# Two ranks in a kernel's opening plan: batch 0's theta earlier on TensorE, the splits of theta's weights later

## The chip, the cores and the metric

The kernel runs on one core of one Trainium2 chip. The metric is the device time in microseconds of one execution. The kernel before the change was run three times: 577.52, 577.86 and 578.83, median 577.86 us. TensorE is called PE here (PEld its weight loads), VectorE DVE, ScalarE ACT, GpSimd POOL, SyncE SP.

## What is computed

Banded attention with 8 heads of 64 dimensions feeds a block that mixes tokens with a learned rotation, for 8 batches of 576 positions:

```
scores = q k^T / 8, masked (heads 0-3: the last 32 positions; heads 4-7: every 4th of the last 128)
x      = softmax(scores) v, heads side by side: (8, 576, 512)
theta  = x w_theta                       # 512 x 512
zr, zi = x cos(theta), x sin(theta)
u      = x + w_tok_r zr + w_tok_i zi     # 576 x 576 each, over tokens
out    = u + relu(u w_ch)                # 512 x 512
```

The result is float32.

## The kernel before

Heads are worked in four pairs `pr`. For each batch and pair, `scores` multiplies q and k in bands, masks, and takes the exponentials (ACT) and the normalization (POOL). `flip` (on PE, batch 0) or `turn` (on DVE, batch 1 on) transposes the probabilities, `pv` multiplies them with v, and `x_evac` copies the result to x, which lies with 128 of the 512 dimensions on the partitions.

Theta is computed for five tiles of tokens, in the order `STS = (4, 0, 1, 2, 3)`; tile 4 has 64 tokens, the others 128. `theta0` does it for batch 0: one float32 product for each of the four pieces `c` of the 512 dimensions, into a PSUM bank named by `TP0`. When the four are done it starts `trig` for the tile. `trig` rounds theta to whole turns on ACT (K, line 787), subtracts them on DVE (line 789), and takes the sine on ACT (line 796). It also starts `natural`, four transposes on PE that bring x to tokens on partitions (xn, line 759). `by_x` multiplies sine and xn on DVE (line 750), `cosine` takes the absolute value (line 698) and the cosine (line 705) on ACT and multiplies again. `zsplit` splits each product into a rounded high part zh (DVE, line 641, or ACT, line 644) and a rest zl (POOL, line 646). There are nine such pieces `kt` for the token product: kt 0 to 3 are from cosines of tiles 0 to 3, kt 4 to 7 from their sines, kt 8 holds both of tile 4.

`token` sums over the nine pieces in the order `KORD = (0, 4, 1, 5, 2, 6, 3, 7, 8)`, three products each (zh and zl with the weights' high part, zh with their low part), for four pieces `d` of the dimensions and two halves `g` of the tokens: eight units. `residual` adds x and splits u. `chan` does the last product in eight more units and `finish` adds the result.

Weights come in as raw pairs of words and are made floats by `unpack` (a clamp on DVE, line 332; ACT, lines 334 and 340, or DVE, line 337; DVE, line 342). Then `split` makes the high part on ACT (line 350) and the rest on POOL (line 352). Theta's weights are used whole for batch 0 (`wth32`), and split (`theta_split`) for the other batches. `theta_split` for piece c may start when all five tiles have used that piece. The channel weights' split lands in the tile where the raw theta weights lay, so `chan_weights` waits for the event `("wc", c)` of `theta_split` (line 386). The token weights' second half (`token_late`) and the channel weights are loaded into tiles that earlier steps give back.

The sine and the exponential need different tables on ACT. The exponentials of batch 1 wait until the last sine or cosine of batch 0 has been issued (event `sin0`, lines 444 and 500), and `table` keeps their order.

The order of the opening (batch 0, and scores, turns, pv and theta of batch 1) is made by the planner `Order` while the program is built. Each step of work is a generator which yields an engine with an estimated cost, or an event to wait for. `run` takes the engine that can start first, and on it, among the steps that are ready by then, the one of lowest rank, and of equal ranks the one started first (line 120). It never leaves an engine idle while a step is ready. A step becomes ready again an engine-dependent latency after its end (0.1 us for PE). A step that is started by another, as `natural` by `trig`, inherits the rank unless it is given one (line 89). What was planned is pinned: each engine executes it in that order. The ranks are in `RANK`. `theta0` adds 0.01 for each tile in STS order (line 966), `trig0` too (line 670), `theta_split` and the token weights 0.01 for each piece, and scores 0.21 for each pair. PE instructions are pinned in every phase; from batch 1's token products on, the other engines' order is left to the compiler's scheduler.

Of the kernel before, what the change touches and what calls it, by code (L numbers as in the profile page):

```python
# [29 lines left out]
EARLY = ("u0", "u1", "u2", "u3", "xh0")  # L30
LATE = ("u3", "xh1", "xh2", "xh3", "xh0")
LATE2 = ("xh2", "xh3", "xh2", "xh3")
RANK = dict(load=6.64, scores0=1.09, flip=0.01, pv0=1.13, pair=.21, theta_unpack=1.54, theta0=5.3, trig0=2.41,
            token_early=2.55, theta_split=6.42, token_late=6.75, chan=2.1, units=2.95, evacuate=4.49,
            scores1=4.02, scores2=7.3, pv1=8.0, theta1=5.96, trig1=7.42)
STS = (4, 0, 1, 2, 3)

# [24 lines left out]
class Order:  # L62
# [17 lines left out]
    def signal(self, event):  # L80
        self.events[event] = self.now

    def go(self, gen, rank=None):
        if not self.live:
            for _ in gen:
                pass
            return
        self.serial += 1
        t = [self.rank if rank is None else rank, self.serial, self.now, gen, None, 0.0]
        self.tasks.append(t)  # L90
        self.advance(t)
# [60 lines left out]
def build(ctx, tc, qT, kT, vw, wth, wtk, wch, maskb, ident, identb, outT):  # L152
# [46 lines left out]
    def give(tag, n):  # L199
        if od.live:  # L200
            signal(("free", tag, n))
# [11 lines left out]
    def load_qk(n):  # L213
        if n >= B * NP:
            return
        b, pr = divmod(n, NP)
        r = yield from take("qk", 2)
        q = ap.tile([128, 2 * NJ, 2 * QB], F32, tag="q", name=f"q{b}_{pr}")
        k = ap.tile([128, S + 32], F32, tag="k", name=f"k{b}_{pr}")
        yield "DMA", dma(2 * S)  # L220
        pin(nc.sync.dma_start(q, qT[b, pr]))
        yield "DMA", dma(S + 32)
        pin(nc.sync.dma_start(k, kT[b, pr]))
        qks[b, pr] = (q, k, r)
        signal(("qk", b, pr))

    def load_va(n):
        if n >= B * NP:
            return
        b, pr = divmod(n, NP)  # L230
        r = yield from take("va", 2)
        va = ap.tile([128, VA, 128], F32, tag="va", name=f"va{b}_{pr}")
        yield "DMA", dma(VA * 128)
        pin(nc.sync.dma_start(va, vw[b, pr, :, :VA]))
        vs["a", b, pr] = (va, r)
        signal(("va", b, pr))

    def load_vb(n):
        if n >= B * NP:
            return  # L240
        b, pr = divmod(n, NP)
        if n == NP - 1:
            r = None
            vb = hp.tile([128, DM], F32R, tag="zl8", name="first_vb").bitcast(F32)
            vb = vb.rearrange("p (a b) -> p a b", b=128)
        else:
            r = yield from take("vb", 1)
            vb = ap.tile([128, NJ - VA, 128], F32, tag="vb", name=f"vb{b}_{pr}", bufs=1)
        yield "DMA", dma((NJ - VA) * 128)
        pin(nc.sync.dma_start(vb, vw[b, pr, :, VA:]))  # L250
        vs["b", b, pr] = (vb, r)
        signal(("vb", b, pr))
# [162 lines left out]
    def on_pe(b, pr):  # L415
        return b == 0 or (b, pr) in ((1, 2), (1, 3), (2, 0), (2, 1))
# [24 lines left out]
    def scores(b, pr):  # L441
# [35 lines left out]
        else:  # L477
            give("qk", rqk)
            go(load_qk(b * NP + pr + 2), RANK["load"])
        if b and on_pe(b, pr):  # L480
# [122 lines left out]
    def pv(b, pr):  # L603
# [18 lines left out]
        if ra is not None:  # L622
            give("va", ra)
            go(load_va(n + 2), RANK["load"])
        if rb is not None:
            give("vb", rb)
            go(load_vb(NP if n == NP - 2 else n + 1), RANK["load"])
        if b:
# [25 lines left out]
    def theta0(st):  # L654
        cs = slice(128 * st, min(128 * st + 128, S))
        n = cs.stop - cs.start
        for c in range(NC):
# [11 lines left out]
            signal(("th0", st, c))  # L669
        go(trig(0, st), RANK["trig0"] + .01 * STS.index(st))  # L670

# [145 lines left out]
    def residual(b, d, g, ps, rel):  # L817
        ts = slice(HS * g, HS * g + HS)
        x = xf[b, d]
        if g == 0:  # L820
            yield from take(f"u{d}", 1, UH.get(d) if b == 0 else None)
            u = hp.tile([128, 2, S], F32R, tag=f"u{d}", name=f"u{b}_{d}")
            uh[b, d], ul[b, d] = u[:, 0], u[:, 1]
        yield "DVE", dve(HS)
        pin(nc.vector.tensor_tensor(x[:, ts], ps, x[:, ts], op=ALU.add))  # L825
        give(*rel)
        yield "ACT", act(HS)
        pin(nc.scalar.copy(uh[b, d][:, ts], x[:, ts]))  # L828
        yield "POOL", pool(HS)
        pin(nc.gpsimd.tensor_tensor(ul[b, d][:, ts], x[:, ts], uh[b, d][:, ts].bitcast(F32), op=ALU.subtract))  # L830
        signal(("u", b, d, g))
# [4 lines left out]
    def token(b, d, g):  # L836
# [15 lines left out]
        signal(("tk", b, d, g))  # L852
        go(residual(b, d, g, ps, rel), RANK["evacuate"])

    def finish(b, e, g, ps, rel):
        ts = slice(HS * g, HS * g + HS)
        x = xf[b, e]
        yield "DVE", dve(HS)
        pin(nc.vector.scalar_tensor_tensor(out=x[:, ts], in0=ps, scalar=0.0, in1=x[:, ts],  # L859
                                           op0=ALU.max, op1=ALU.add))  # L860
        give(*rel)
        signal(("out", b, e, g))
        if b == B - 1:
            pin(nc.sync.dma_start(outT[b, e][:, ts], x[:, ts]))
        elif g == 1:
            yield "DMA", dma(S)
            pin(nc.sync.dma_start(outT[b, e], x))

    def chan(b, e, g):
# [7 lines left out]
        for c in range(NC):  # L877
# [3 lines left out]
            for l, r in ((wchs[c][0], uh[b, c]), (wchs[c][0], ul[b, c]), (wchs[c][1], uh[b, c])):  # L881
                pe(nc.tensor.matmul(ps, l[:, cs], r[:, ts], start=(n == 0), stop=(n == 3 * NC - 1)))  # L882
                n += 1
        go(finish(b, e, g, ps, rel), RANK["evacuate"])

# [173 lines left out]
```

## Time and profile before

| what | value |
|---|---|
| median of three runs | 577.86 us |
| the profiled execution's own time | 577.82 us |
| its span, first to last instruction | 576.0 us |
| mean granted TensorE clock | 0.988 |
| busy: PE, DVE, ACT, POOL | 550.5, 378.0, 345.2, 222.2 us |

Busy time is given as a share of a stretch of time. In the timeline views each row is a start, a length, an engine, a line of the kernel, an operation, what it writes and reads, and how many such instructions were merged; brackets hold the idle time of the engine ahead of it and what ended that. The granted clock is the share of full TensorE speed.

### The profile page before, as it was taken

What the parts mean: (1) busy time and instruction counts of PE and PEld (TensorE: products, weight loads), DVE (VectorE), ACT (ScalarE), POOL (GpSimd) and SP (SyncE); (2) the same over time, 40 slices, a digit from 0 to 9 for tenths busy, and PEclk for the clock granted to TensorE, in tenths of its full rate; (3) what the DMA queues carried; (4) which work ended last, traced back from release to release, by engine and by line L of the source; (5) the groups of instructions that cost most, each with busy time, mean ns of one, the idle gap of its engine ahead of it and who ended that gap; (6) DMA issues with size and microseconds to landing.
All of it is one profiled execution on the core that took longest, in us unless ns stands there. A gap on an engine that the chain in (4) does not pass through costs nothing.

```text
span 576.0 us, 13996 instructions
## 1 busy us (share of the span) xinstructions
PE 550.5 (96%) x5464; PEld 501.6 (87%) x5464; DVE 378.0 (66%) x1156; ACT 345.2 (60%) x939; POOL 222.2 (39%) x206
## 2 busy tenths in 40 slices
PE   5997799999999999999999999999999999999997
PEld 4744688879999899988999899988999899989997
DVE  3879798865666668756776768756775767445112
ACT  1498967768555784369555785359556695266110
POOL 2228855525224352226324253226323353325220
PEclk9999699899999999999999999999999999999999
DMA  8991437601747046540746146550747123321002
GB/s 303 400 368 28 165 105 245 216 0 63 231 150 193 32 162 210 169 127 20 268 143 172 64 148 202 181 136 11 252 146 190 69 83 102 77 89 65 18 1 83
DMA packets 45586, 81.91 MB, mean 142 GB/s; under 512 B 3920, under 2 KB 19024, under 8 KB 45520
## 3 DMA queue, kind: packets, MB, share of 16 engines
q1 hardware_dynamic: 45520, 81.02, 43.7%
q8 instruction: 43, 0.70, 0.5%
q14 instruction: 23, 0.19, 0.1%
HBM read 64.49 MB, written 16.52 MB: 141 GB/s over the span
## 4 chain that ended last, share of the span: by engine, by line
DVE 34%; ACT 30%; PE 25%; issue 5%; POOL 2%; DMA 2%; SPq 0%; ACTq 0%; POOLq 0%; DVEq 0%
DVE pt L525 16%; PE y L850 11%; ACT P L504 11%; PE c L882 6%; PE th L685 3%; DVE P L409 3%; ACT K L698 3%; ACT K L787 3%; DVE xh L599 3%; ACT th L796 2%; ACT zh L644 2%; DVE xq L729 2%; DVE K L789 2%; ACT cos L705 2%; ACT x L581 2%
## 5 line engine op out<-in xcount | busy, mean ns | idle before, releaser
L830 POOL TENSOR_TENSOR u<-x,u 128x288 fp32r<-128x288 f32 x64 | 54.7, 858 | 184.6 <-ACT u L828 184.6
L525 DVE STREAM_TRANSPOSE pt<-P 32x288 f32<-32x288 f32 x224 | 105.1, 469 | 12.0 <-POOL P L510 8.9
L882 PE MATMUL c<-u,late_wc 128*128 128x288 f32 x768 | 110.2, 296 | 2.8 <-DVE x L859 2.8
L882 PEld LDWEIGHTS c<-u,late_wc 128*128 128x128 f32 x768 | 106.0, 188 | 6.8 <-DVE x L859 4.0
L850 PE MATMUL y<-wtkh,zh 128*128 128x288 f32 x288 | 90.3, 314 | 1.1 <-ACT zh L644 1.1
L850 PE MATMUL y<-wtkh,zl 128*128 128x288 f32 x288 | 86.2, 299 | 4.0 <-POOL zl L646 4.0
L646 POOL TENSOR_TENSOR zl<-g,zh 128x512 fp32r<-128x512 f32 x40 | 52.3, 1316 | 97.5 <-ACT zh L644 84.5
L504 ACT ACTIVATE P<-P,mx 128x64 f32<-128x64 f32 x216 | 72.0, 335 | 25.8 <-DVE mx L498 25.8
L850 PE MATMUL y<-wtkl,zh 128*128 128x288 f32 x288 | 85.9, 298 | 0.0
L828 ACT CAST u<-x 128x288 fp32r<-128x288 f32 x64 | 26.9, 429 | 86.2 <-DVE x L825 85.5
L685 PE MATMUL th<-wthh,xh 128*128 128x512 f32 x224 | 74.8, 395 | 0.3 <-DVE g L784 0.3
L850 PE MATMUL y<-late_wt_b,zh 128*128 128x288 f32 x320 | 68.1, 297 | 0.0
L825 DVE TENSOR_TENSOR x<-y,x 128x288 f32<-128x288 f32 x64 | 28.1, 448 | 53.6 <-PE y L850 53.5
L850 PEld LDWEIGHTS y<-wtkh,zl 128*128 128x128 f32 x288 | 55.1, 191 | 4.7 <-POOL zl L646 4.7
L850 PEld LDWEIGHTS y<-wtkh,zh 128*128 128x128 f32 x288 | 54.9, 191 | 4.7 <-ACT zh L644 2.3
L850 PE MATMUL y<-late_wt_a,zh 128*128 128x288 f32 x256 | 56.3, 301 | 0.0
L850 PEld LDWEIGHTS y<-wtkl,zh 128*128 128x128 f32 x288 | 55.1, 191 | 0.3 <-issue 0.3
L510 POOL TENSOR_TENSOR P<-P,sm 128x576 f32<-128x576 f32 x32 | 37.5, 1172 | 41.1 <-DVE sm L508 18.1
L850 PEld LDWEIGHTS y<-late_wt_b,zh 128*128 128x128 f32 x320 | 51.4, 189 | 0.3
L685 PEld LDWEIGHTS th<-wthh,xh 128*128 128x128 f32 x224 | 42.0, 188 | 9.2 <-DVE g L784 0.6
L850 PE MATMUL y<-late_wt_b,zl 128*128 128x288 f32 x160 | 47.4, 296 | 0.0
L581 ACT COPY x<-o 128x576 f32<-128x576 f32 x32 | 29.4, 919 | 28.4 <-PE o L617 19.1
(108 smaller groups left out, 1106.3 us busy)
## 6 DMA issues: line engine op xcount, KB each, us to landing
q<-in_qT_dram SPq DMA_DIRECT2D x32, 576.0 KB, 5.2
va<-in_vw_dram SPq DMA_DIRECT2D x30, 320.0 KB, 3.2
k<-in_kT_dram SPq DMA_DIRECT2D x28, 304.0 KB, 5.5
out_dram<-x SPq DMA_DIRECT2D x28, 288.0 KB, 2.4
vb<-in_vw_dram SPq DMA_DIRECT2D x29, 256.0 KB, 3.8
xd<-xq SPq DMA_DIRECT2D x24, 288.0 KB, 5.1
xn<-xd SPq DMA_DIRECT2D x24, 256.0 KB, 3.4
st_wtk<-in_wtk_dram SPq DMA_DIRECT2D x8, 576.0 KB, 8.8
```

The lines of the kernel that those rows point to most:

```text
L409: pin(nc.vector.tensor_tensor_reduce(out=P[:, n], in0=ps[:, n - g0], in1=mskb[:, mask_of(pr, n)], op0=ALU.add, op1=ALU.max, scale=1.0, sca ...
L504: table(nc.scalar.activation(P[:, n], P[:, n], AF.Exp, bias=mx[:, n:n + 1], scale=SCALE, accum_out=sm[:, n:n + 1]))
L510: pin(nc.gpsimd.tensor_tensor(P, P, sm.unsqueeze(2).to_broadcast([128, NJ, BW]), op=ALU.mult))
L525: pin(nc.vector.transpose(pmats[b, pr][k0:k0 + QB, :, hh, QB * e:QB * e + QB], P[p0:p0 + QB, :, QB * o:QB * o + QB]))
L581: pin(nc.scalar.copy(dst, src))
L646: pin(nc.gpsimd.tensor_tensor(lo, z, hi.bitcast(F32), op=ALU.subtract))
L685: pe(nc.tensor.matmul(pt, l, r, start=(n == 0), stop=(n == 3 * NC - 1)))
L825: pin(nc.vector.tensor_tensor(x[:, ts], ps, x[:, ts], op=ALU.add))
L828: pin(nc.scalar.copy(uh[b, d][:, ts], x[:, ts]))
L830: pin(nc.gpsimd.tensor_tensor(ul[b, d][:, ts], x[:, ts], uh[b, d][:, ts].bitcast(F32), op=ALU.subtract))
L850: pe(nc.tensor.matmul(ps, l[:, cs], r, start=(n == 0), stop=(n == 3 * NK - 1)))
L882: pe(nc.tensor.matmul(ps, l[:, cs], r[:, ts], start=(n == 0), stop=(n == 3 * NC - 1)))
```

## The change

Two entries of `RANK` get other values. `theta0` goes from 5.3 to 2.39: above 2.39 are now `trig0` (2.41, with the transposes of `natural`), `token_early` (2.55), `units` (2.95, the token and channel products) and `scores1` (4.02 and up), which were below 5.3. `theta_split` goes from 6.42 to 8.74: `load` (6.64), `token_late` (6.75), `scores2` (7.3), `trig1` (7.42) and `pv1` (8.0 to 8.63) are now below it. Nothing else differs; the same instructions are issued in another order.

```diff
-RANK = dict(load=6.64, scores0=1.09, flip=0.01, pv0=1.13, pair=.21, theta_unpack=1.54, theta0=5.3, trig0=2.41,
-            token_early=2.55, theta_split=6.42, token_late=6.75, chan=2.1, units=2.95, evacuate=4.49,
+RANK = dict(load=6.64, scores0=1.09, flip=0.01, pv0=1.13, pair=.21, theta_unpack=1.54, theta0=2.39, trig0=2.41,
+            token_early=2.55, theta_split=8.74, token_late=6.75, chan=2.1, units=2.95, evacuate=4.49,
             scores1=4.02, scores2=7.3, pv1=8.0, theta1=5.96, trig1=7.42)
```

## The prediction

> **What bounds the kernel now.** I read the page's busy table first, then the busy time by stage, then the order of time on TensorE, ScalarE and VectorE in the stage that the change touches.
>
> ```profile
> PE 550.5 (96%) x5464; PEld 501.6 (87%) x5464; DVE 378.0 (66%) x1156; ACT 345.2 (60%) x939; POOL 222.2 (39%) x206
> ```
>
> Over the whole span TensorE (PE) is the bound. By stage (columns: stretch, its length, busy us of PE, PEld, DVE, ACT, POOL, granted clock, DMA share, GB/s) it is not the same everywhere:
>
> ```profile
> 50.00:69.90 19.90, 13.78 (x98) 10.58 (x97) 16.39 (x50) 18.44 (x54) 17.52 (x15) 0.78 0.41 136
> 69.90:120.00 50.10, 47.05 (x539) 42.52 (x537) 44.94 (x101) 34.86 (x119) 28.41 (x25) 0.95 0.48 163
> 143.00:560.00 417.00, 414.22 (x4083) 390.61 (x4083) 265.44 (x898) 244.60 (x692) 151.30 (x145) 1.00 0.42 129
> ...
> 37.82:61.28 23.46, 19.55 (x116) 10.90 (x116) 21.66 (x48) 21.28 (x39) 18.06 (x13) 0.92 0.40 139
> ```
>
> From 143 us on PE is idle 2.8 us in 417 (417.00 - 414.22): whatever PE arrives early at that point is kept to the end, one for one. Before it, from 50 to 69.9, PE is idle 6.1 us of 19.9 at a granted clock of 0.78, while ScalarE (ACT) is busy 18.4 of 19.9. That is the stage of batch 0's sines and cosines, and the change works there. From 69.9 to 120 VectorE (DVE, 44.9 of 50.1) and PE (47.1) are both nearly full; this stage can be started earlier but hardly shortened.
>
> TensorE's order of time in the first stage (start us, us, line, names, entries; a theta product L667 shows as two entries):
>
> ```profile
> 36.30 2.21 PE L667 MATMUL th<-st_wth,x 128*64 128x512 f32 x4 [0.56 <-ACT x L581]
> 38.34 0.60 PE L759 MATMUL xn<-idt,x 128*64 128x128 f32 x4
> 38.78 1.97 PE L667 MATMUL th<-st_wth,x 128*128 128x512 f32 x4
> 40.59 0.60 PE L759 MATMUL xn<-idt,x 128*128 128x128 f32 x4
> 41.02 1.97 PE L667 MATMUL th<-st_wth,x 128*128 128x512 f32 x4
> 42.91 0.80 PE L468 MATMUL s<-k,q 128*64 128x64 f32 x20
> 43.65 2.07 PE L667 MATMUL th<-st_wth,x 128*128 128x512 f32 x4
> 45.56 0.60 PE L759 MATMUL xn<-idt,x 128*128 128x128 f32 x4
> 45.99 3.77 PE L667 MATMUL th<-st_wth,x 128*128 128x512 f32 x8
> 49.60 0.60 PE L759 MATMUL xn<-idt,x 128*128 128x128 f32 x4
> ...
> 52.09 1.06 PE L667 MATMUL th<-st_wth,x 128*128 128x512 f32 x2
> ...
> 53.38 1.06 PE L667 MATMUL th<-st_wth,x 128*128 128x512 f32 x2
> ...
> 56.52 0.41 PE L850 MATMUL y<-wtkh,zl 128*128 128x288 f32 x1 [1.52 <-POOL zl L646]
> ...
> 66.79 0.40 PE L850 MATMUL y<-wtkh,zl 128*128 128x288 f32 x1 [1.11 <-POOL zl L646]
> ```
>
> The reader should see two things. Theta's last product ends at 54.4 because transposes, scores and token products stand between its pieces. And from 50 us on PE waits for z (zl from GpSimd, POOL), which comes out of the sine chain.
>
> **The change part by part.** *Theta forward on TensorE.* From 36.30 on there are 28 theta entries, so 14 products, of 3.77/4 = 0.94 us: 13.2 us. The new ranks step by 0.01: theta of the tiles in STS order stands at 2.39 to 2.43, each tile's transposes at 2.41 to 2.45 (they inherit trig's rank, line 89), and line 120 gives a tie to the task that was there first. So the transposes of tile 4 come behind theta of tiles 4, 0 and 1, but ahead of tiles 2 and 3; those of tile 0 only ahead of tile 3. One tile's next product becomes ready 0.1 us after its last, in the planner's terms, so products of two tiles alternate. This gives: five products, transposes of tile 4 at 41.0; two products, transposes of tile 0 at 43.4 (one transpose group takes 45.99 - 45.56 = 0.43); six products, transposes of tile 1 at 49.5; one product, theta ends at 36.3 + 13.2 + 3 x 0.43 = 50.8. Against 54.4 that is 3.6 us earlier. The first half of scores (0.74 us at 42.91), tokens and the transposes of tile 2 come after it.
>
> Are the transposes missed? They move from 38.34, 40.59 and 45.56 to 41.0, 43.4 and 49.5. Their readers are the products x times sine on DVE:
>
> ```profile
> 41.65 0.69 DVE L750 TENSOR_TENSOR g<-xn,g 64x512 f32<-64x512 f32 x1
> ...
> 43.77 0.69 DVE L750 TENSOR_TENSOR g<-xn,g 128x512 f32<-128x512 f32 x1
> ...
> 50.59 0.68 DVE L750 TENSOR_TENSOR g<-xn,g 128x512 f32<-128x512 f32 x1
> ```
>
> Ended at 41.5, 43.9 and 49.9 the transposes meet these starts to within 0.1 us. They cost nothing as long as the sines themselves don't come sooner; when that cover is gone each microsecond counts on DVE.
>
> *What the earlier theta is worth.* Not 3.6 us, because PE does not set this stage:
>
> ```profile
> 50.70 0.45 ACT L350 CAST wtkh<-st_wtk 128x288 fp32r<-128x288 f32 x1 [1.48 <-DVE st_wtk L342]
> ...
> 51.59 0.65 ACT L350 CAST wthh<-st_wth 128x512 fp32r<-128x512 f32 x1
> ...
> 55.95 0.58 ACT L787 ACTIVATE K<-th 128x512 int32<-128x512 f32 x1
> ...
> 58.39 0.63 ACT L796 ACTIVATE g<-K 128x512 f32<-128x512 f32 x1 [0.68 <-DVE K L789]
> ...
> 60.66 0.71 ACT L705 ACTIVATE K<-K,halfpi 128x512 f32<-128x512 f32 x1
> ...
> 62.03 1.28 ACT L504 ACT_TABLE_LOAD   x1
> ```
>
> The rounding K of the last tile starts at 55.95, 1.5 us after its theta is done, and ACT is not idle in front of it: it stands in ACT's queue. The last cosine starts at 60.66; behind it comes the table load at 62.03 and all exponentials of batch 1, which wait for the last sine or cosine (line 500). From 37.82 (first K) to 61.28 ACT is busy 21.28 of 23.46 us. What can leave this stretch: the idle 2.18 us, and the four casts of theta's weights, which the second edit ranks last.
>
> *Theta's split behind all else.* It moves four casts on ACT and four subtractions on POOL:
>
> ```profile
> L350 ACT CAST wthh<-st_wth 128x512 fp32r<-128x512 f32 x4 | 2.6, 654 | 0.0
> L352 POOL TENSOR_TENSOR wthl<-st_wth,wthh 128x512 fp32r<-128x512 f32 x4 | 5.3, 1323 | 0.0
> ```
>
> The planner never leaves an engine idle while something is ready, so a cast can still fill a short gap early; it yields only where the unpacking of the second half of the token weights (6.75 to 6.79) is ready, now ranked ahead. I take two of the four casts as leaving the stretch: 1.3 us. Bounds: none (0, or the token unpacking takes the same place) and all four (2.6). Of the idle time the 0.68 us wait for L789 of the last tile goes, since that tile's theta and K come sooner and L789 has a place further ahead in DVE's queue. The 1.48 us wait hangs on a slow DVE operation of the token weights, not on theta; I take half, 0.7, between none and all. The sum is 0.7 + 0.7 + 1.3 = 2.7 us, between 0.7 and the full 2.18 + 2.6 = 4.8.
>
> Is DVE able to follow? In the same stretch it is busy 21.66 of 23.46. It is relieved, since masking of batch 1's first scores moves behind with the scores, but it holds the gain below 4 us. On POOL the split's products stand among the zl ones; two 1.3 us pieces in front of the last zl vanish, which agrees with zl following ACT's casts.
>
> One cost in this stage is contention of DVE with POOL:
>
> ```profile
> L332 DVE TENSOR_SCALAR st_wtk<-st_wtk 128x576 f32<-128x576 f32 x6 | 4.2, 703 | 0.0
> L332 DVE TENSOR_SCALAR st_wtk<-st_wtk 128x288 f32<-128x288 f32 x2 | 2.9, 1456 | 0.0
> ```
>
> Half as many words take twice as long, in a stage where POOL is full. Against 0.70 for the larger form a meeting costs at least 0.8 us. If packing the zl products closer makes two more such meetings, 1.6 of the 2.7 us are lost. I keep that as the low end of the gain (1.1) and take no more meetings than before as the likelier, since the number of operations on both engines is unchanged. [...]
>
> *Who waits for theta's split.* The channel weights overwrite its raw tile (line 386), and batch 1's theta needs the split.
>
> ```profile
> 69.80 1.30 POOL L352 TENSOR_TENSOR wthl<-st_wth,wthh 128x512 fp32r<-128x512 f32 x1
> ...
> 95.99 0.66 ACT L350 CAST late_wc<-st_wch 128x512 fp32r<-128x512 f32 x1
> ...
> 71.00:96.00 25.00, 23.95 (x319) 21.45 (x320) 22.40 (x50) 18.33 (x62) 14.30 (x14) 1.00 0.47 163
> ```
>
> The last piece ends at 71.1 and the first reader is at 95.99. In these 25 us ACT has 6.7 and POOL 10.7 us free, which hide 2.6 and 5.3. I cost this at nothing; without the cover up to 5.3. No DMA issue changes its rank. The raw channel loads wait for token tiles that come free no later than before.
>
> *To the end.* The exponentials of batch 1 start 2.7 us sooner, the DVE transposes that follow (first at 69.9) too, and the 50 us behind are bound by the same work as before. So the profiled execution of 577.82 us (span 576.0) becomes 575.1; the median of the runs shown is 0.04 above the profiled one, so 575.2. A measurement of this kernel tells about 0.2% (1.2 us) from no change.
>
> **The rivals.** *Nothing gained* (577.8): ACT's gaps are refilled by the token weights' unpacking, which now outranks the split, and the sine chain stays as long. For it: two such operations already stand in front of the table load, and ACT's total work is unchanged. Against it: theta is available 3.6 us sooner, so sines can take places they could not. *Scores too late* (slower, 579.4): scores of batch 1 now come behind theta and share TensorE's in-order queue with token products that wait for z.
>
> ```profile
> 60.12 2.19 PE L468 MATMUL s<-k,q 128*64 128x64 f32 x36
> 62.24 0.61 PE L850 MATMUL y<-wtkh,zh 128*128 128x288 f32 x1
> ...
> 63.61 0.44 PE L850 MATMUL y<-wtkh,zl 128*128 128x288 f32 x1
> ```
>
> If these 36 products stand behind the token step now at 62.24 to 63.85 instead of ahead of it, masks and exponentials come 1.6 us later than now, and DVE's transposes with them. It decides once the exponentials are ready later than the table load. Against it: scores fill PE's waits for z, and theta's last tile frees its bank earlier. *Everything gained, and the clock* (573.0): all 4.8 us leave.
>
> ```profile
> 58.00:60.00 2.00, 1.04 (x8) 0.72 (x4) 1.52 (x10) 1.61 (x3) 2.00 (x2) 0.50 0.78 252
> 60.00:62.00 2.00, 2.00 (x37) 1.89 (x36) 1.71 (x7) 2.00 (x4) 2.00 (x3) 0.50 0.96 366
> ```
>
> PE runs here at half its clock; fewer waits would keep it up, though PE waits for z right after, so little of that would show. [...] *Split too late*: 583.1, if the channel weights wait for all 5.3 us.
>
> **How the numbers follow.** Forecast 0.48 (574.0 to 576.7), everything gained 0.08, nothing 0.17, scores too late 0.24, split too late 0.03. Faster by over 0.2%: 0.48 + 0.08 = 0.56; the same 0.17; slower 0.24 + 0.03 = 0.27. The likeliest time is 575.2. The range runs from 572.6, which takes in most of everything gained, to 579.8, which takes in most of the slower case; the split too late and the tails are left out, under 0.2.
>
> **What would show it.** Right: theta's last product near 50.8, the last cosine near 58, the table load near 59.3, the first DVE transpose near 67.2, and PE's arrival at batch 1's tokens (143 now) 2.7 us sooner. Wrong: the table load not moved though theta is early (ACT refilled); the table load early but the first transpose not (scores or DVE late); or both early and the 143 us mark unmoved, so that the 50 us behind gave it back.

## The result, and the profile after

| | before | after |
|---|---|---|
| median of six runs | 578.23 us (576.97 to 579.68) | 582.44 us (580.84 to 583.65) |
| profiled execution | 577.82 us, span 576.0 | 583.65 us, span 581.9 |
| mean granted clock of the profiled execution | 0.988 | 0.979 |

The change makes the kernel slower: ratio 1.0075, 95% interval 1.0059 to 1.0090, which is 3.4 to 5.2 us. The forecast was 575.2, and the measured time lies beyond even the slower end of its range, 579.8. The profiled execution of the changed kernel lies 1.2 us above its median, and its clock is the lowest of the six (the others have 0.982 to 0.988), so its trace shows more of the loss than a typical one would.

Busy time by stage of the changed kernel (columns as in the prediction: stretch, length, busy us of PE, PEld, DVE, ACT, POOL, granted clock, DMA share, GB/s):

```profile
50.00:69.90 19.90, 14.46 (x118) 12.07 (x117) 17.83 (x60) 16.47 (x49) 13.07 (x11) 0.75 0.49 166
69.90:120.00 50.10, 43.34 (x496) 38.70 (x495) 42.93 (x89) 35.44 (x121) 28.62 (x27) 0.90 0.49 163
143.00:560.00 417.00, 414.28 (x4083) 390.63 (x4082) 268.25 (x903) 247.06 (x695) 151.68 (x145) 1.00 0.42 130
```

The last row is as before. In the middle row PE is busy 3.7 us less in the same 50 us (47.05 before), executes 496 products instead of 539, and its clock is 0.90 instead of 0.95. So the greater part of the loss sits in the stage that the prediction passed over as "bound by the same work".

**The opening.** Order of time on PE, then on ScalarE, of the changed kernel:

```profile
50.24 1.07 PE L667 MATMUL th<-st_wth,x 128*128 128x512 f32 x2
```

```profile
48.91 0.66 ACT L350 CAST wthh<-st_wth 128x512 fp32r<-128x512 f32 x1
...
51.46 0.46 ACT L350 CAST wtkh<-st_wtk 128x288 fp32r<-128x288 f32 x1 [1.36 <-DVE st_wtk L342]
...
53.45 0.73 ACT L334 ACTIVATE st_wtk<-st_wtk 128x576 f32<-128x576 f32 x1
54.08 0.57 ACT L787 ACTIVATE K<-th 128x512 int32<-128x512 f32 x1
...
55.08 0.72 ACT L340 ACTIVATE st_wtk<-st_wtk 128x576 uint32<-128x576 uint32 x1
...
59.77 0.74 ACT L334 ACTIVATE st_wtk<-st_wtk 128x576 f32<-128x576 f32 x1 [1.22 <-DVE st_wtk L332]
60.41 0.71 ACT L705 ACTIVATE K<-K,halfpi 128x512 f32<-128x512 f32 x1
...
61.65 1.28 ACT L504 ACT_TABLE_LOAD   x1
...
63.96 0.71 ACT L340 ACTIVATE st_wtk<-st_wtk 128x576 uint32<-128x576 uint32 x1
```

Theta ends at 51.3, near the predicted 50.8 (54.4 before). Three of the four split casts have left the stretch (one is left, at 48.91). But the unpacking of the second token weights (L334, L340) stands in their places, at 53.45, 55.08 and 59.77, the last with a wait of 1.22 us in front of it and the last cosine (L705) behind it. The table load comes at 61.65, 0.4 us sooner, not 2.7. Another unpacking stands among the exponentials at 63.96. On VectorE:

```profile
65.74 1.23 DVE L498 TENSOR_SCALAR mx<-mx 128x9 f32<-128x9 f32 x1
...
70.89 0.95 DVE L525 STREAM_TRANSPOSE pt<-P 32x288 f32<-32x288 f32 x2 [1.02 <-POOL P L510]
```

The scaling of the row maxima at 65.74 holds up the exponentials, and the first transpose comes at 70.89: 1.0 us later than before (69.88), not 2.7 sooner.

**Behind the opening.** Scores go into banks of PSUM. A bank comes free when ScalarE has taken the exponentials (L485) of the scores that it held, and the next masks (L424) are the first to write into it. PE's waits for a score bank, before and after (L424 masks, L468 scores, L850 the first token product of batch 1):

```profile
82.47 0.31 PE L424 MATMUL s<-mskb,idb 128*128 128x64 bf16 x5 [1.04 <-ACT P L485]
...
85.12 0.69 PE L468 MATMUL s<-k,q 128*64 128x64 f32 x16
...
101.51 0.30 PE L424 MATMUL s<-mskb,idb 128*128 128x64 bf16 x2 [1.95 <-ACT P L485]
...
105.85 0.69 PE L468 MATMUL s<-k,q 128*64 128x64 f32 x16
...
144.21 0.40 PE L850 MATMUL y<-wtkh,zh 128*128 128x288 f32 x1
```

```profile
83.10 0.31 PE L424 MATMUL s<-mskb,idb 128*128 128x64 bf16 x5 [2.81 <-ACT P L485]
...
87.22 0.69 PE L468 MATMUL s<-k,q 128*64 128x64 f32 x16
...
105.43 0.43 PE L424 MATMUL s<-mskb,idb 128*128 128x64 bf16 x2 [3.58 <-ACT P L485]
...
111.12 0.69 PE L468 MATMUL s<-k,q 128*64 128x64 f32 x16
...
150.04 0.40 PE L850 MATMUL y<-wtkh,zh 128*128 128x288 f32 x1
```

The waits grow from 1.04 + 1.95 = 3.0 to 2.81 + 3.58 = 6.4 us. Not all of this is a later bank. PE reaches the first mask at 80.29 (83.10 - 2.81), where it was 81.43 before, so it is 1.1 us ahead there; the bank comes 0.6 us later, and the wait holds both. Behind each wait, the same work takes longer too: from the mask to the second half of the scores 4.12 us (87.22 - 83.10) instead of 2.65, and 5.69 instead of 4.34. PE is 2.1 us behind the kernel before at the first second half, 3.9 at the second mask, 5.3 at its scores and 5.8 at the first token product of batch 1. The longer work is the clock, first in the windows behind the two waits after, then behind the two before, where the first wait is followed by full clock:

```profile
83.10:87.30 4.20, 4.20 (x40) 3.50 (x41) 2.44 (x9) 4.07 (x16) 1.05 (x1) 0.59 0.73 267
105.40:111.20 5.80, 5.77 (x40) 5.03 (x41) 4.96 (x11) 3.43 (x13) 3.04 (x3) 0.52 0.40 152
```

```profile
82.40:85.20 2.80, 2.73 (x40) 2.27 (x41) 1.91 (x6) 2.80 (x13) 1.63 (x2) 1.00 0.78 276
101.50:106.00 4.50, 4.49 (x39) 3.79 (x40) 3.30 (x11) 2.37 (x11) 1.25 (x1) 0.62 0.87 286
```

Why the second bank comes late is seen on VectorE, before and after:

```profile
91.07 0.43 DVE L332 TENSOR_SCALAR st_wch<-st_wch 128x512 f32<-128x512 f32 x1
...
98.17 0.49 DVE L430 TENSOR_REDUCE mx<-s 128x5 f32<-128x320 f32 x1
...
99.67 0.17 DVE L438 TENSOR_SCALAR mx<-mx 128x5 f32<-128x5 f32 x1
```

```profile
83.57 0.42 DVE L332 TENSOR_SCALAR st_wch<-st_wch 128x512 f32<-128x512 f32 x1
...
99.06 0.48 DVE L430 TENSOR_REDUCE mx<-s 128x5 f32<-128x320 f32 x1
...
100.43 0.69 DVE L342 SCALAR_TENSOR_TENSOR st_wch<-st_wch 128x512 uint32<-128x512 uint32 x1
101.03 0.42 DVE L332 TENSOR_SCALAR st_wch<-st_wch 128x512 f32<-128x512 f32 x1
...
102.48 0.80 DVE L438 TENSOR_SCALAR mx<-mx 128x5 f32<-128x5 f32 x1
```

The exponentials need the row maximum (L430) and its scaling (L438). They were 1.5 us apart (99.67 - 98.17) and are now 3.4: two steps of the channel weights' unpacking stand between them (1.06 us) and one more pair of transposes (0.99). The scaling itself takes 0.80 us instead of 0.17, and on ScalarE one more step of the unpacking, at 103.24, stands in front of the exponentials (103.79). With theta's split last, the third of the late token weights is split sooner (its cast starts at 76.23, not 83.78), the load of the first channel weights is issued at 78.9, not 86.2, their first clamp runs at 83.57, not 91.07, and this unpacking, of rank 2.1, goes ahead of everything of the scores. The first bank is another case. Its wait ends at 83.10, ahead of the first clamp; the scaling that its exponentials need comes at 81.17 instead of 80.54, behind transposes that began 1.0 us later. From batch 1's tokens to the end nothing differs: 576.0 - 144.21 = 431.8 and 581.9 - 150.04 = 431.9.

### The profile page after: what moved, and what is told of

It reads as the page before. It is cut to its first block, busy times and chain, and to the rows that moved or that the text cites. A ratio compares the mean times of both kernels' runs of the same rounds, so it can differ in the third digit from the quotient of the medians.

```text
span 581.9 us, 13993 instructions
## 1 busy us (share of the span) xinstructions
PE 552.5 (95%) x5464; PEld 504.1 (87%) x5464; DVE 382.0 (66%) x1156; ACT 345.3 (59%) x939; POOL 219.7 (38%) x206
## 4 chain that ended last, share of the span: by engine, by line
PE 31%; DVE 31%; ACT 29%; DMA 4%; issue 4%; POOL 1%; SPq 0%; ACTq 0%; DVEq 0%
DVE pt L525 14%; PE y L850 13%; ACT P L504 11%; PE c L882 7%; DVE P L409 3%; PE th L667 3%; PE th L685 3%; ACT K L698 3%; DVE xh L599 2%; ACT th L796 2%; ACT K L787 2%; ACT zh L644 2%; DVE xq L729 2%; DVE K L789 2%; PE o L617 2%
## 5 line engine op out<-in xcount | busy, mean ns | idle before, releaser
L830 POOL TENSOR_TENSOR u<-x,u 128x288 fp32r<-128x288 f32 x64 | 54.4, 853 | 180.3 <-ACT u L828 180.3
L850 PE MATMUL y<-wtkh,zh 128*128 128x288 f32 x288 | 90.5, 314 | 1.3 <-ACT zh L644 1.3
L850 PE MATMUL y<-wtkh,zl 128*128 128x288 f32 x288 | 86.5, 300 | 1.9 <-POOL zl L646 1.9
L850 PE MATMUL y<-wtkl,zh 128*128 128x288 f32 x288 | 86.3, 300 | 0.0
L646 POOL TENSOR_TENSOR zl<-g,zh 128x512 fp32r<-128x512 f32 x40 | 51.4, 1293 | 91.2 <-ACT zh L644 80.4
L828 ACT CAST u<-x 128x288 fp32r<-128x288 f32 x64 | 26.8, 428 | 83.6 <-DVE x L825 82.9
L850 PE MATMUL y<-late_wt_b,zh 128*128 128x288 f32 x320 | 69.0, 300 | 0.0
L825 DVE TENSOR_TENSOR x<-y,x 128x288 f32<-128x288 f32 x64 | 28.2, 449 | 53.1 <-PE y L850 53.0
L850 PEld LDWEIGHTS y<-wtkh,zh 128*128 128x128 f32 x288 | 55.3, 192 | 3.8 <-ACT zh L644 1.6
L850 PEld LDWEIGHTS y<-wtkh,zl 128*128 128x128 f32 x288 | 55.4, 192 | 2.3 <-POOL zl L646 2.3
L850 PE MATMUL y<-late_wt_a,zh 128*128 128x288 f32 x256 | 56.4, 302 | 0.0
L850 PEld LDWEIGHTS y<-wtkl,zh 128*128 128x128 f32 x288 | 55.5, 193 | 0.0
L850 PEld LDWEIGHTS y<-late_wt_b,zh 128*128 128x128 f32 x320 | 51.9, 191 | 0.4
L850 PE MATMUL y<-late_wt_b,zl 128*128 128x288 f32 x160 | 47.6, 297 | 0.0
L581 ACT COPY x<-o 128x576 f32<-128x576 f32 x32 | 29.4, 918 | 28.2 <-PE o L617 23.5
## 6 DMA issues: line engine op xcount, KB each, us to landing
q<-in_qT_dram SPq DMA_DIRECT2D x32, 576.0 KB, 5.1
st_wtk<-in_wtk_dram SPq DMA_DIRECT2D x8, 576.0 KB, 8.6
```

Of the source, the lines that this page charges most:

```text
L581: pin(nc.scalar.copy(dst, src))
L646: pin(nc.gpsimd.tensor_tensor(lo, z, hi.bitcast(F32), op=ALU.subtract))
L850: pe(nc.tensor.matmul(ps, l[:, cs], r, start=(n == 0), stop=(n == 3 * NK - 1)))
```

## The experiments

Executions of whatever kernel differ ahead of the first rounding K (L787), which starts at 36.2 to 38.8 us, so marks in the opening are compared from there. The table has marks of each profiled execution in us (T: table load behind the sines; V: first transpose on DVE; B: first token product of batch 1), each as a difference of two rows of its timeline, the last of B and the span. The ratio is to the kernel before on the same chip.

| kernel | K to T | K to V | V to B | B to end | ratio, 95% interval |
|---|---|---|---|---|---|
| before | 24.2 | 32.1 | 74.3 | 431.8 | 1 |
| changed | 23.5 | 32.7 | 79.2 | 431.9 | 1.0075 (1.0059 to 1.0090) |
| theta only | 22.9 | 32.3 | 76.4 | 431.6 | 1.0052 (1.0038 to 1.0065) |
| split only | 26.6 | 34.3 | 76.6 | 433.2 | 1.0075 (1.0061 to 1.0088) |
| theta at 2.5 | 24.3 | 32.5 | 78.9 | 431.9 | 1.0069 (1.0056 to 1.0082) |
| channel weights later | 23.6 | 32.8 | 75.5 | 431.9 | 1.0039 (1.0025 to 1.0052) |
| changed, cleared stage | 22.1 | 33.1 | 76.5 | 433.9 | 1.0074 (1.0057 to 1.0091) |
| before, cleared stage | 23.6 | 32.7 | 78.4 | 433.1 | 1.0120 (1.0095 to 1.0146) |
| changed, row max in one step | 23.6 | 32.8 | 75.3 | 431.9 | 1.0051 (1.0031 to 1.0071) |
| before, row max in one step | 24.2 | 32.1 | 76.5 | 433.2 | 1.0076 (1.0055 to 1.0096) |
| opening after, rest before | 23.5 | 32.4 | 74.3 | 431.9 | 1.0020 (1.0004 to 1.0037) |
| opening before, rest after | 24.2 | 32.1 | 78.9 | 431.9 | 1.0070 (1.0049 to 1.0090) |
| changed, spare products | 23.5 | 32.4 | 75.8 | 431.8 | 1.0045 (1.0024 to 1.0067) |
| changed, max and channel | 23.5 | 32.8 | 82.0 | 432.8 | 1.0167 (1.0143 to 1.0190) |

In five of these kernels the time from B to the end is 1.0 to 2.1 us longer as well, so V to B alone is not their whole price. The marks are of one execution each, the ratio of all.

**The two ranks one by one, and theta's exact place.** My first theory was that the split's lateness alone costs, by way of the channel weights, and that theta's place is harmless or a gain; the rival, that theta's place costs.

```
 theta only:    theta0=2.39, theta_split=6.42
 split only:    theta0=5.3,  theta_split=8.74
 theta at 2.5:  theta0=2.5,  theta_split=8.74
```

> Only theta's rank is changed (2.39), the split keeps 6.42. Theory A (the late split lets the channel weights come early, and their unpacking, of rank 2.1, stands in VectorE's order in front of the row maxima and transposes of batches 1 and 2, so that TensorE waits longer for score banks and then runs at half clock): the unpacking is not early here, so 576 to 578.5 us, with TensorE waiting under 3.5 us in total at L424. Theory B (theta forward is what costs, since transposes, scores and token products come later): 581 to 584 us.

> Only the split's rank is changed (8.74), theta keeps 5.3. Theory A: the unpacking of the first channel weights starts near 83 us as in the changed kernel (91 before), TensorE waits 5 us or more at L424, 581 to 584 us. Theory B: as before, 577.5 to 579 us.

> The split at 8.74 and theta at 2.5: theta comes behind all transposes, but in front of scores and token products. Theory A: the transposes do not matter, 581 to 584 us. Theory B, if the transposes are what costs: 577 to 579.5 us.

Theta alone: 581.11 against 578.36, so 2.2 to 3.8 us slower. The theory fell here. Its table load is the earlier one (22.9), but V to B is 2.1 longer, and not by score banks: their waits are 1.01 and 1.32 us, and the longest wait is for batch 0's residual, ahead of the channel products:

```profile
118.21 1.09 PE L882 MATMUL c<-u,late_wc 128*128 128x288 f32 x3 [2.29 <-DVE x L825]
```

Split alone: 582.96, as slow as both together, yet its bank waits are only 1.21 and 0.47 us, so the place that was expected was wrong. The channel weights did come early, as the theory has it: their first clamp is at 81.20 (at 94.55 with theta alone moved). The loss stands elsewhere: 2.4 us at the table load already, waits for v from a DMA (1.60), for the channel weights' split (0.84) and for a residual (1.73), and 1.4 us behind B. Theta at 2.5, where batch 0's transposes go ahead of it again and scores and tokens don't: 582.34, no better. The moved transposes are not what costs. Three orders, three sets of waits, and prices that overlap (2.2 to 3.8, 3.5 to 5.1 and 3.2 to 4.7 us): this spoke for a loss in the whole order behind the opening, not in one moved step.

**The channel weights' rank.**

```diff
-token_late=6.75, chan=2.1,
+token_late=6.75, chan=7.35,
```

> The changed kernel with the rank of the channel weights at 7.35 instead of 2.1, so that their unpacking gives way to the transposes of batch 1 (4.0 to 4.7) and the row maxima of batch 2's first scores (7.3). Theory A: TensorE's waits at L424 fall from 6.4 to about 3 us and the time to 577 to 579 us. Theory B: 582 us as the changed kernel, since theta's place is unchanged.

580.16 against 578.36: 1.4 to 3.0 us slower than before, so some 2 of the 4.2 us are back, fewer than expected. The two bank waits fall from 6.4 to 4.1 us:

```profile
83.05 0.31 PE L424 MATMUL s<-mskb,idb 128*128 128x64 bf16 x5 [1.81 <-ACT P L485]
...
102.45 0.30 PE L424 MATMUL s<-mskb,idb 128*128 128x64 bf16 x2 [2.32 <-ACT P L485]
```

Only the second bank is sooner, by 3.0 us. The first comes at the same time as in the changed kernel (83.05 and 83.10); its wait is shorter because PE reaches it 1.0 us later (81.24 and 80.29).

**Is theta's early end worth anything in the sine stage?** In both kernels what refills ACT's gaps was made to wait for the last sine or cosine:

```diff
 def unpack(...):                          # ahead of the clamp, line 328
+    if name == "wtk1_":
+        yield None, "sin0"
 def theta_split(c):                       # ahead of the split, line 361
+    yield None, "sin0"
```

> The changed kernel, in which the splits of theta's weights and the unpacking of the token weights' second half also wait for the event that the last sine or cosine of batch 0 has been issued, so that neither can fill a gap in the sine stage. Theory (refilled: what leaves ScalarE's and VectorE's queues in the sine stage is replaced by other weights' work, so the earlier theta gains nothing there): the table load starts at 59.5 us or sooner, against 61.65 in the changed kernel. Rival (the sine chain itself, or the late transposes, bound the stage): 61 us or later. The whole time is not the point, 578 to 584 us, since weights come later.

> The kernel before with the same two waits. Theory: with the stage cleared, theta's place shows: the table load at 60.5 to 62 us, 1.5 us or more behind the same kernel with theta in front. Rival (theta's place is worth nothing in this stage at all): within 0.5 us of the other.

First rounding and table load, of the changed kernel and then of the kernel before, both with the cleared stage:

```profile
36.55 0.63 ACT L790 ACTIVATE K<-th 64x512 int32<-64x512 f32 x1
...
58.68 1.28 ACT L507 ACT_TABLE_LOAD   x1
```

```profile
38.13 0.58 ACT L790 ACTIVATE K<-th 64x512 int32<-64x512 f32 x1
...
61.70 1.28 ACT L507 ACT_TABLE_LOAD   x1
```

The table loads lie 3.0 us apart, but 1.6 of it was there at the first rounding; from there on it is 22.1 against 23.6. So theta's earlier end is worth 1.4 us in an undisturbed stage, a little less than the 1.5 expected, and 0.7 (23.5 against 24.2) with the refilling: refilling takes half. The gain does not survive. What was put off stands on DVE next, in the changed kernel with the cleared stage:

```profile
61.60 3.63 DVE L334 TENSOR_SCALAR st_wtk<-st_wtk 128x576 f32<-128x576 f32 x4
...
68.41 1.35 DVE L344 SCALAR_TENSOR_TENSOR st_wtk<-st_wtk 128x576 uint32<-128x576 uint32 x1 [0.56 <-ACT st_wtk L342]
```

These and sixteen transposes in one row behind them make PE wait 3.55 us at 76.5 for the transposed probabilities. Another new wait, 3.28 us at 116.7, is for a residual (L828) ahead of the channel products. Times: 581.86 and 584.70 against 577.45, both slower than before.

**The row maximum and its scaling planned as one step,** so that nothing comes between them on DVE:

```diff
-        yield "DVE", dve((g1 - g0) * BW)
+        yield "DVE", dve((g1 - g0) * BW) + (170 if b else 0)
         pin(nc.vector.tensor_reduce(mx[:, g0:g1], ps, ...
...
-            yield "DVE", 170
             pin(nc.vector.tensor_scalar(mx[:, g0:g1], mx[:, g0:g1], -SCALE, ...
```

> The changed kernel with the two halves of the row maxima of batches 1 and 2 (reduction, line 430, and scaling, line 438) planned as one step, so that no transpose or unpacking comes between them in VectorE's queue. Theory (TensorE waits for score banks because the scaling stands behind other work on VectorE): the waits at L424 fall from 6.4 to 3 us or less, with less half clock behind them, 579 to 580.5 us. Rival (VectorE's total work in the stage sets the pace, whatever its order): 582 to 583 us.

> The kernel before with the row maxima planned as one step. Theory: the waits at L424 fall from 3.0 us to 1 or less, 576 to 577.5 us. Rival: 578 to 579 us.

In the changed kernel one bank wait is left, 1.94 us at 83.1, and the time is 580.36 against 577.45: 1.8 to 4.1 us slower than before. In the kernel before, the same edit takes both bank waits away and still costs 4.4 us (581.82, where 576 to 577.5 was expected): waits of 1.69 for v, 1.14 and 2.04 for the channel weights' split are new, and 1.4 us more stand behind B. So a removed wait is no gain by itself: each edit re-plans all in-order queues behind it.

**Opening and rest apart.** The planner was given lists of its own steps, for each engine, and takes the next of the list instead of the lowest rank. The list is one kernel's order up to a planned start (that of the first transposes of batch 1) and the other kernel's order for all steps behind it.

```diff
-                t = min((t for t in ready if t[4] == eng and t[2] <= at), key=lambda t: (t[0], t[1]))
+                if eng in self.orders:
+                    want = self.orders[eng].pop(0)
+                    t, = (t for t in ready if t[4] == eng and (t[6], t[7]) == want)
...
```

> On every engine the steps that the changed kernel's plan starts in the opening (up to the point where batch 1's first turn has been planned) stand in the changed kernel's order, and all steps behind it in the order of the kernel before. Theory P (the loss is made behind the opening, by the re-planned order there): the banks' waits at L424 fall from 6.4 to 3.5 us or less, batch 1's tokens come at 143.5 to 145.5 instead of 150.0, and the time is 577 to 579. Rival O (the opening itself costs, since the first turn comes at 70.9 instead of 69.9): 579.5 to 582, with the first turn again near 70.9. Rival L (any order that was not timed loses somewhere): over 579, with a new wait of 1.5 us or more that neither kernel has.

> The reverse: the opening in the order of the kernel before, all steps behind it in the order of the changed kernel. Theory P (the loss is made behind the opening): 581 to 583, first turn near 69.9 and yet 5 us or more of waits at L424. Rival O (the opening itself costs): 577 to 579. Rival L (any order that was not timed loses somewhere): 580 to 585, and not by the waits at L424.

Bank waits and batch 1's tokens, first of the opening after with the rest before, then of the reverse (L424 is L441 here, L850 is L867):

```profile
83.78 0.31 PE L441 MATMUL s<-mskb,idb 128*128 128x64 bf16 x5 [1.54 <-ACT P L502]
...
102.89 0.30 PE L441 MATMUL s<-mskb,idb 128*128 128x64 bf16 x2 [2.02 <-ACT P L502]
...
145.03 0.40 PE L867 MATMUL y<-wtkh,zh 128*128 128x288 f32 x1
```

```profile
83.49 0.31 PE L441 MATMUL s<-mskb,idb 128*128 128x64 bf16 x5 [2.64 <-ACT P L502]
...
104.60 0.30 PE L441 MATMUL s<-mskb,idb 128*128 128x64 bf16 x2 [1.93 <-ACT P L502]
...
148.82 0.40 PE L867 MATMUL y<-wtkh,zh 128*128 128x288 f32 x1
```

This settles where. With the changed opening and the old order behind it the time is 578.82 against 577.81 (ratio 1.0004 to 1.0037), V to B is 74.3 as before, and the bank waits are 3.56 us, a hair over the 3.5 expected. With the old opening and the changed order behind it the time is 582.27 (1.0049 to 1.0090), and V to B is 78.9. The changed opening costs about 1 us (0.2 to 2.1) and the changed order behind it about 4 (2.8 to 5.2); the two ratios add up to 1.0090, the upper end of the whole's interval. In the first of the two kernels the splits of theta's weights come as late as in the changed one (casts from 74.91 on), so their lateness by itself is not what costs. And the bank waits are not the whole of it: in the second they are 4.57 us, under the 5 expected and well under the changed kernel's 6.4, at nearly the same price.

**The clock.** In the changed kernel PE was kept busy during the two bank waits:

```diff
+                spare = {(1, 3, 0): 18, (2, 1, 0): 24}.get((b, pr, g0), 0)
...
+                    for n in range(spare):
+                        pe(nc.tensor.matmul(pw[:, :256], zero, mskb[:, :4], start=True, stop=True))
...
                 mask_on_pe(ps, pr, g0, g1)
```

> The changed kernel with 18 and 24 spare products (zeros by the masks, into an unused bank, never read) on TensorE just ahead of the two masks that wait for their bank, about 2.3 and 3.1 us of work in waits of 2.8 and 3.6 us; 42 products of 0.13 us. Theory C (the waits cost twice, once by themselves and once by the half clock behind them): the clock stays near 1.00 from 80 to 112, the stretches from the masks to the next scores shrink from 4.1 and 5.7 us to 2.7 and 3.0 to 4.3, and the time falls from 582.4 to 579.5 to 581. Rival: the clock stays up but TensorE then waits for the next late step (theta of batch 1, channel weights), and the time is 581.8 to 583. Third: the clock falls all the same, and the time is 582 to 583.5.

```profile
78.50 2.14 PE L469 MATMUL warm<-mskb,zero 128*128 128x256 bf16 x18
81.30 0.30 PE L426 MATMUL s<-mskb,idb 128*128 128x64 bf16 x5 [0.66 <-ACT P L493]
...
83.95 0.69 PE L476 MATMUL s<-k,q 128*64 128x64 f32 x16
...
98.79 2.79 PE L469 MATMUL warm<-mskb,zero 128*128 128x256 bf16 x24
101.42 0.30 PE L426 MATMUL s<-mskb,idb 128*128 128x64 bf16 x2
```

The spare products took 0.12 us each (2.14 / 18 and 2.79 / 24; 0.13 was expected). The first wait is as long as it was (81.30 - 78.50 = 2.80 with the spare work in it), but the stretch behind it takes 2.65 us instead of 4.12, the second wait has shrunk to what the spare work covers, and the clock is 1.00 from 70.9 to 144. V to B falls from 79.2 to 75.8. The median is 580.91 against 577.81, a ratio of 1.0045 where the changed kernel has 1.0075: about 1.7 us back, though the intervals (1.0024 to 1.0067 and 1.0059 to 1.0090) overlap a little. In this execution theory C held: without the half clock the same work takes 1.5 us less, so a wait of this kind is paid twice. How much of the 1.7 us of the median is the clock's stays open, for the profiled execution took 578.52 us, 2.4 below the median, at a mean clock of 0.994; five of the other six took 580.35 to 581.90 at 0.985 to 0.991, where the changed kernel has 0.979 to 0.988.

**Both partial remedies together.**

```diff
-token_late=6.75, chan=2.1,
+token_late=6.75, chan=7.35,
...
-            yield "DVE", 170
```

The last line stands for the whole edit of the row maximum shown above.

> Both partial remedies together in the changed kernel: channel weights' rank 7.35 and the row max with its scaling planned as one step, which gave back 2.3 and 2.1 us one by one. If they are two separate losses: 577.5 to 579. If they are the same loss twice: 579.5 to 580.5, with waits at L424 under 2 us. If a later channel product takes the place (theory of a loss moved, not removed): 581 or more, with waits at L825 (by this kernel's lines 824) of 2 us or more.

587.33 against 577.81. The loss was moved, not removed, and grew: the channel weights' split (L350) is now too late for the channel products. The residual (L824), where the wait was expected, is the lesser one.

```profile
113.46 1.45 PE L881 MATMUL c<-u,late_wc 128*128 128x288 f32 x9 [1.11 <-DVE x L824]
120.23 0.85 PE L881 MATMUL c<-u,late_wc 128*128 128x288 f32 x2 [5.32 <-ACT late_wc L350]
```

No kernel here was faster than the kernel before; the nearest is the changed opening with the old order behind it.

## Why the prediction was wrong

- *Theta forward on PE*: right. It ended at 51.3 (50.8 predicted), and the moved transposes were not missed: of their readers on VectorE only the last tile's waits for its transposes, 1.09 us where it was 0.77 before, and theta at 2.5, with transposes ahead, was no faster.
- *What the earlier theta is worth*: mis-sized. The 2.7 us were 0.7 from the first rounding to the table load, and 1.4 where the stage was cleared. Of the sum's three terms the wait of 0.68 went as forecast. The wait of 1.48, of which half was taken, stayed at 1.36. Three split casts, not two, left the stretch (about 2.0 us for the 1.3 taken), but the bound of "none (0, or the token unpacking takes the same place)" was the one that held: that unpacking outranks the split now, and the planner never leaves an engine idle. VectorE, taken to be relieved, was busy 9.93 of the 10 us from 50 to 60 (9.05 before), and the last unpacking on ScalarE waited 1.22 us for it, ahead of the last cosine. The rival *nothing gained* had this mechanism right. At the first transpose even that was gone (0.7 us later from the first rounding on), since another unpacking and a slow scaling of the maxima stood among the exponentials.
- *Theta's split behind all else*: costed at nothing, for its readers come 25 us later. The readers did not wait, and the opening with the late splits in it cost about 1 us. But the sentence "the raw channel loads wait for token tiles that come free no later than before" covered one side alone: they came free sooner (the load was issued 7.3 us sooner), and the first channel unpacking moved from 91.07 to 83.57, ahead of the scores' work on DVE.
- *To the end*: this is the step that failed. "The 50 us behind are bound by the same work as before" holds for the amount of work, not for its order. Both ranks re-plan every in-order queue up to batch 1's tokens; that rest alone, behind the old opening, costs 2.8 to 5.2 us of the 3.4 to 5.2. PE is the bound of the whole kernel, yet in this stage it depends on chains through two score banks, and its waits for them grew by 3.4 us, with the half clock on top.
- *Scores too late*, the slower rival, had the sign and not the mechanism: the last of the scores ended at 61.1 instead of 62.3, and their last mask on VectorE was 0.6 us later (64.4 and 63.8), a small part of the loss. *Split too late* did not occur. *Everything gained, and the clock* counted the clock as a gain in the sine stage, from fewer waits. There PE was idle 5.4 us of 19.9 (6.1 before), and the clock was 0.75 (0.78 before). It became a loss 20 to 50 us behind that stage, where it stayed at 1.00 when spare products filled the bank waits.

How the 4 us behind the opening divide is settled only in part. Three treatments (channel weights later, maximum in one step, the clock held up) each give back 1.4 to 2.1 us by the ratios and 3.4 to 3.9 us of V to B in the profiled executions. The second measure is larger, at least in part because the changed kernel's profiled execution lies 1.2 us above its median and that with spare products 2.4 below. They were not shown to add: the first two together lost more than the change itself. Later residuals and channel products ahead of batch 1's theta were seen in the waits at L825 of theta only, split only and theta at 2.5, but not taken apart.

## What to carry to other kernels

In this kernel a rank in the planner was not a local move: what was made later let something else come earlier, and every in-order queue behind it was dealt anew. So a change in the opening needs a forecast for the order of the whole planned stretch, or a plan that is held fixed behind the place that is changed. Where engines are filled whenever anything is ready, time taken out of a stage is refilled by the next in rank unless that one is held back, and holding it back moves it onto another path. Replaying one kernel's order behind another's opening is a direct way to find which part pays.

## What the runs showed of the hardware

Waits of TensorE of some 2 us were in part followed by half its clock. Waits of 1 us or more that ended between 80 and 110 us, with the clock of a stretch behind them where one was read:

| kernel | wait, us | ended at, us | stretch, us | granted clock in it |
|---|---|---|---|---|
| before | 1.04 | 82.47 | 82.4 to 85.2 | 1.00 |
| before, cleared stage | 1.25 | 104.54 | 100 to 110 | 1.00 |
| before, row max in one step | 1.69 | 105.51 | 100 to 110 | 1.00 |
| changed, max and channel | 1.76 | 81.72 | 81 to 86 | 0.66 |
| channel weights later | 1.81 | 83.05 | 80 to 90 | 1.00 |
| theta at 2.5 | 1.90 | 105.52 | 103 to 110 | 1.00 |
| changed, row max in one step | 1.94 | 83.08 | 80 to 90 | 0.83 |
| before | 1.95 | 101.51 | 101.5 to 106 | 0.62 |
| before, cleared stage | 2.10 | 90.54 | 90.5 to 96 | 1.00 |
| channel weights later | 2.32 | 102.45 | 100 to 110 | 0.83 |
| theta at 2.5 | 2.63 | 84.74 | 80 to 90 | 0.83 |
| changed | 2.81 | 83.10 | 83.1 to 87.3 | 0.59 |
| changed | 3.58 | 105.43 | 105.4 to 111.2 | 0.52 |

Of these, the waits up to 1.69 us were followed by a clock of 1.00. Of the ten of 1.76 us or more seven were followed by a lower one; 1.81, 1.90 and 2.10 us were not. In the sine stage of the kernel before the clock was 0.50 from 58 to 62 us, and no wait of TensorE between 50 and 62 us was longer than 1.52. Within a cut the clock was 0.50 (84 to 87 us in the changed kernel, 102 to 105 in the kernel before). If it was so in each cut, the clock of a stretch gives the length: behind 83.10 in the changed kernel (1 - 0.59) x 4.20 / 0.5 = 3.4 us, behind 101.51 in the kernel before (1 - 0.62) x 4.50 / 0.5 = 3.4, behind 81.72 with max and channel (1 - 0.66) x 5 / 0.5 = 3.4, and in the three stretches of 10 us at 0.83 (1 - 0.83) x 10 / 0.5 = 3.4. The seventh, at the 3.58 us wait of the changed kernel, began 1.3 us before the wait ended and lasted twice that:

```profile
104.15:111.00 6.85, 5.57 (x38) 4.95 (x37) 6.15 (x14) 4.48 (x22) 2.84 (x3) 0.50 0.49 165
```

So by estimate a cut of 3.4 us costs up to 1.7 us where PE is full; 1.5 was measured behind 83.10 (4.12 against 2.65 with spare products).

A scaling of nine words for each partition (L498) took 1.23 us at 65.74 in the changed kernel, while GpSimd's last subtraction of the sine stage (L646) ran (65.25, 1.69 us), and 0.16 us at 60.26, when GpSimd was idle (59.41 to 61.71). The exponential at 67.00 waited 0.82 us for it.
